# Attention and feed-forward kernel: the first batch's scales, exps and loads rearranged

## The chip, the cores and the metric

The kernel runs on one core of a Trainium2 chip. The core has five engines that run side by side, each through its own list of instructions in order: TensorE (PE in the profile, its weight loads PEld) multiplies matrices and writes to PSUM, VectorE (DVE) and ScalarE (ACT) read PSUM and work on tiles, GpSimd (POOL) works on tiles in SBUF alone here, and SyncE (SP) issues DMAs. ScalarE and GpSimd issue DMAs too; the profile marks an instruction in which an engine only issues as ACTq, POOLq or SPq. Engines wait for each other and for DMAs through semaphores.

The metric is device time in microseconds (us) of one execution; smaller is better.

## What is computed

The reference is a linear attention with an exponential feature map, followed by a gated feed-forward layer:

```python
batch, n_heads, seq, head_dim = (8, 8, 576, 64)
d_feat = 128
def phi(x):
    proj = np.einsum('bhsd,df->bhsf', x, w_phi)
    proj = proj - np.max(np.abs(proj), axis=-1, keepdims=True)
    return np.concatenate([np.exp(proj), np.exp(-proj)], axis=-1)
q_p, k_p = (phi(q), phi(k))
kv = np.einsum('bhsf,bhsd->bhfd', k_p, v)
z = np.sum(k_p, axis=2)
num = np.einsum('bhsf,bhfd->bhsd', q_p, kv)
den = np.einsum('bhsf,bhf->bhs', q_p, z)[..., None] + 1e-06
attn_out = (num / den).astype(np.float32)
x = np.ascontiguousarray(attn_out.transpose(0, 2, 1, 3)).reshape(B * S, H * D)
gate = np.maximum(x @ w_gate, 0.0)
val = x @ w_val
out = (gate * val @ w_out).astype(np.float32)
```

There are 4608 tokens, a model width of 512 and a hidden width of 1536. The row maximum that phi subtracts can be kept out of the big exps: the kernel computes exp(proj) and exp(-proj) from PSUM, and puts exp(-m) and exp(m), one number a row and sign, into v instead ("scales"). The column of ones that gives z becomes a column of the scales themselves.

## The kernel before, in words

**Tiles.** A batch has 8 heads of 576 rows: 512 rows in four chunks of 128, and a tail of 64 that is put together over heads, batches or both. A k item is two heads of one batch (four items a batch, `k_item`), plus one tail item (`k_tail`). For each item, pieces follow each other: kT (TensorE transposes k, VectorE copies it to SBUF as tT), krows (TensorE multiplies with w_phi, which lies twice in the tile w2, once for each half of the partitions), kmax (VectorE's row maximum, L247, and ScalarE's two small exps of it, the tile ek, L291), kexp (ScalarE's exps of the projection, the tile kp, L279), vs (GpSimd multiplies v by ek for both signs, L251, and casts ek into the last column, L257), and kv (TensorE sums over the rows, L323 and L331, with a copy to SBUF, L339). For the tail there is kmv in place of vs: GpSimd first makes ekm, ek with one half of the partitions zeroed (L308).

Queries go through qT, qrows (projection both ways round, L357 and L265), qexp (L372 to L375), qmax (row maximum and ScalarE's small cq, L385), num (TensorE times kv, L402, and five small VectorE steps up to a reciprocal r, with GpSimd's xu = u times r, L419) and x (a transpose of xu into xT). The feed-forward of batch g then runs in half steps: wv (L457, copied to val_sb by ScalarE, L466), wg (L457, joined by VectorE, L470), and at last out (L483). For the first batch a half step takes one chunk of 128 tokens and a third of the hidden width.

**Order.** Every piece is added to a plan with engine costs, needs and buffers, but what is emitted comes from ORDER, a list written into the file: numbers of pieces with the PSUM banks that they take, and entries such as z22:0, which stand for n times 128 columns of dummy matmuls on zeros (`keep_busy`, L999), into bank 0. The costs that stand beside the pieces are read by an ordering program that is not part of the kernel; `Plan.order` reads ORDER and nothing else. The order of the instructions on each engine, DMA issues included, is thus the order of ORDER, with the code ahead of it first. Piece 0 is the load of the first q, 1 and 2 the first thirds of the value and gate weights; 43 is the first kT.

**First loads.** Ahead of ORDER, SyncE issues two loads of k for heads 0 to 3 (in fp32), the k tail and the v tail; ScalarE issues one half of w_phi into wf and then v in four loads of two heads (L163); GpSimd issues the other half of w_phi straight into w2, makes the identity matrices, and loads k of heads 4 to 7 (late_k, in bf16, L1028). ScalarE then casts wf into w2 (L1036). Items 0 and 1 of the first batch run through `k_crosswise`: VectorE's maximum of one half of the heads beside ScalarE's exps of the other half.

```python
    for u in range(NU):
        if u < 2:
            load_kqv(0, "kn", k, nc.sync, FP32, slice(2 * u, 2 * u + 2))
        load_v(0, 2 * u, 2 * u + 2, nc.scalar)
    load_first_tail(0)
    load_tail(inputs["vt", 0], 0, 1, v, nc.sync)
```

Of the kernel before, what the change touches and what calls it, by code (L numbers as in the profile page):

```python
# [8 lines left out]
FP32 = mybir.dt.float32  # L9
# [37 lines left out]
ORDER = """z22:0 43:76 48:5 44:6 45 z6:4 49:0 z14:2 53:5 0 50 z12:4 54:2 65:7 3 59:6 4 56 1 5 z9:4 66:4 46 67  # L47
68 60:0 61 62 51 55 z56:7 70:4 77 69 84:5 52:6 63 71:02 72 7 11 73 47:7 z9:4 102:6 108:5 114:4 64:2
103:0 9 78:63 104 57 80 8 2 97:5 17 58:2 79 109:3 110 10 74:52 98:6 75:2 111 99 81:52 15 z15:3 76:4
105 82:3 126:2 120:5 85:03 87 139:2 100 86 533:7 88:53 121:0 525:2 6 83:7 89 90 541:2 122 16 526:7  # L50
13 115:3 527:5 101 106 152 123 107:2 18 170 116 117 91:67 168 112 124 528:5 542:7 171 92:6 113:0
94:51 95:2 535:7 543:6 127:30 129 536:7 118 12 128 544:2 177 130:50 96:7 93:3 131 534:4 119:2 125:7
140:53 14 132 142 529:2 133:70 539:1 162 134:4 136:32 537:0 141 538:7 530:1 545:0 189 137:7 20 546:4
21 143:52 153 144 163:0 145 531:7 547:4 164 135:2 19 552:3 166 165 138:5 172:6 173 540:2 553 149:45
554 167 169 150:0 146:12 183 175 174 548:5 549:4 532:3 154:60 155 550 156 147:5 551 221 184:2 22
190:0 178:6 555:5 556 558:4 186 179 180 229 191 185 557 559 187 151:6 192 148:7 157:23 176:5 560
561:3 158:76 195 196:40 197 567:2 24 583:3 181 193 188:6 198 208 159:7 182:4 23 223 241 160:5 562:0
199:61 200 242:3 201 194:5 243 563:0 25 26 584:1 568:2 244 28 575:7 230:5 224:0 222 565:2 573:3 231
225 205:47 566:2 574:3 235 226 232 564:7 206:4 577:2 260 202:30 245 273 576:1 579:7 203:2 227 580:0
236:5 289 209:31 238 211 204 578:7 233 585:0 210 569:1 237 570:2 591:7 291 207 29 212:53 213 239  # L60
581:1 214 571:2 33 298 572:3 215:45 582:6 228:1 246:2 247 30 218:35 240:1 219:4 592 216:2 234:1 283
220 593 292 248:53 284:1 249 217 586 587 310 250 304 588:7 251:35 285 290 252 594:0 595 253 589 286
27 254:65 596 257:34 255:5 590 597:6 598:4 258:7 603:5 287 305:0 342 307 256 261:26 31 263 613:4 262
161 306 609:5 604:6 316 308 614:7 615:4 299:0 264:26 265 266 610:5 605:4 356 300 34 601:6 302 301
274 602:7 35 616:5 259 270:62 32 309:3 617:4 267:75 271:0 618:1 607:6 272 608:2 599:7 311:0 329
275:35 313 277 600:2 611:7 276 312 288 619:5 303:6 606:2 394 620:7 268:0 612:1 293:2 317:46 295
624:0 318 627:1 269 628 319 294 625 320:62 321 357:4 412 410 314 629 626 343 322 296 358 278:23 344
297:6 279:71 350 315:0 39 280:3 639:6 359 323:20 630:1 37 360 637:3 326:07 324:6 631 345:4 351:2 38
347 632 362 352 621:0 327:7 622 635:6 623 281:1 325 633:7 346 634:6 638:0 353 419 354 640:1 330:46
331 653:0 332 645:1 348 654:2 36 646:3 355:0 333:16 363:4 334 335 636:3 647:0 643:6 413 42 364  # L70
339:73 328 644:2 411 365 649:6 361:3 648:7 366 340:0 336:12 655:6 651:7 425 337:0 381 395 349:5 341
652:6 396:13 426:5 397 641:7 398 427 656:0 663:4 642:7 368 428 367:3 650:2 414:0 369:52 664 666:7
338 416 463 667 41 431 370 665 371 689:2 668 420:5 515 422 415 372:03 374 373 421 657:2 660:7 450
661 691:3 669:4 378:56 423 375:01 376:3 662 658 379:4 40 659 687:1 404 399:03 670:2 690:1 405:6
382:42 407 477 417 384 683:0 671:1 429 406 383 692:2 688:3 408 400:01 681:2 684:3 672:1 675:2 385:64
432:0 386 673:3 424:2 387 433 434 682:4 418:5 377 388:36 465 679:7 674:2 464 677:4 391:30 437 389:1
380 676:2 685:7 680:0 471 430:1 435 392:7 686:6 409 390 393 678:5 483 478:3 480 438:60 693:2 694 439
699:5 440 436:0 695 484:6 479 282 441:30 481 700 702:2 442 443 701 485 696:0 486 705:1 703 401:3
447:45 444:67 697 402:1 704 445:3 698 709:7 706:4 707:5 472:6 451:02 474 453 708:4 452 516 710:5
719:2 473 448:3 482:4 713:5 723:0 454:61 466:3 502 456 489 455 724:5 720:0 446 717:1 467 711:2 714:5  # L80
457:01 460:67 449 468 475 469 712:2 715:5 458:1 487 461:0 718:3 470:4 727:7 490:15 491 716:4 732:0
725:7 492 733 488:1 721:2 476:1 493:35 462 459 494 728:7 729:2 726:1 722:7 403 730 495 738:1 496:73
731 745:4 497:3 498 499:56 747:2 743:7 734 500:6 503:24 735:7 741:0 736 504 739 740 505 737 506:52
742:4 746:7 744:0 507 508 748:1 509:45 510:0 749:6 751:7 750:3 759:2 760:1 512:07 513:6 752:5 757:4
753:7 761:6 755:0 758:7 756:1 517:24 518 519 768:0 763:1 501 511 771:7 754:6 762:5 764:4 769 774:3
514 520:21 775 521:65 522:4 765:1 772 776 770 777:2 799:6 766 781:0 767 773 779:0 778:6 800:7 780:5
523:6 787:4 782:7 788:3 793:2 783:1 784:0 794:7 524 797:6 789:5 791:7 798:6 785:0 792:7 813:1 790:0
786:2 795:1 804:0 801:7 796:6 802 805 806 810:1 807:2 803 811 823:0 812 817:3 808 809 829:7 814:6
818:5 824:7 815:6 816:0 827:7 819:1 828:0 835:2 830:1 821:0 836:7 831:6 820:5 822:7 833:6 834:0
825:7 826:1 832:0 837:2 838 846:3 839 847:7 843:6 848:7 840:5 841 844 845 842"""  # L90
# [6 lines left out]
def kernel(  # L97
# [23 lines left out]
    P = 128  # L121
# [55 lines left out]
    def load_tail(t, b, nb, src, eng):  # L177

        for hh in range(2):
            for bb in range(nb):  # L180
                eng.dma_start(
                    out=t[SM * hh : SM * (hh + 1), bb],
                    in_=src[b + bb, hh::2, SF:S, :].rearrange("u p d -> p u d"),
                )
# [64 lines left out]
    def scale_v(dst, src, ek):  # L249

        nc.gpsimd.tensor_tensor(  # L251
            dst[:, :, :, 0:D],
            src[:, :, None, :].to_broadcast([P, *dst.shape[1:3], D]),
            ek[:, :, :, None].to_broadcast([P, *dst.shape[1:3], D]),
            op=ALU.mult,
        )
        nc.gpsimd.tensor_copy(dst[:, :, :, D], ek)  # L257
# [15 lines left out]
    def k_exps(st, n, at, pars=slice(0, 2)):  # L273

        if "kp" not in st:
            st["kp"] = st["pool"].tile([P, 2, 2, 4, F], BF16, name="kp")
        kp = st["kp"][:, :, :, at : at + n]
        for s, sign in ((0, 1.0), (1, -1.0)):
            nc.scalar.activation(kp[:, s, pars], st["rows"][:, pars], AF.Exp, scale=sign)  # L279

    def k_max(st, n, pars=slice(0, 2)):

        if "m" not in st:
            st["m"] = sb_s.tile([P, 8], FP32, name="mk")[:, 0 : 2 * n]
        m = st["m"].rearrange("p (j i) -> p i j", i=2)
        row_max(m[:, pars], st["rows"][:, pars])

    def k_scales(st, n):
        st["ek"] = sb_s.tile([P, 8, 2], FP32, name="ek", bufs=8)[:, 0 : 2 * n]
        for s, sign in ((0, -1.0), (1, 1.0)):  # L290
            nc.scalar.activation(st["ek"][:, :, s], st["m"], AF.Exp, scale=sign)  # L291

    def k_crosswise(st):

        for par in range(2):
            k_max(st, 4, slice(par, par + 1))
            k_exps(st, 4, 0, slice(1 - par, 2 - par))
        k_scales(st, 4)

    def k_values(st, b, u):  # L300
        vs = st["vs"] = sb_k.tile([P, 8, 2, E], BF16, name="vs")
        vn = inputs["vn", b][:, 2 * u : 2 * u + 2].rearrange("p h c d -> p (h c) d")
        scale_v(vs, vn, st["ek"])

    def k_values_tail(st, b, at):

        ekm = sb_s.tile([P, NU, 2, 2], FP32, name="ekm", bufs=2)
        nc.gpsimd.tensor_tensor(  # L308
            ekm,
            st["ek"][:, at : at + NU, :, None].to_broadcast([P, NU, 2, 2]),  # L310
            half[:, None, None, :].to_broadcast([P, NU, 2, 2]),
            op=ALU.mult,
        )
# [3 lines left out]
    def k_kv(st, b, u, copy):  # L317
# [21 lines left out]
        copy(kv.rearrange("p h s e -> p (h s e)"), pk[:, 0 : 4 * E])  # L339
# [265 lines left out]
    def k_pieces(rank, st, start, ops, needs, take, name, banks, late=(), n=4, at=0, wide=True):  # L605
# [12 lines left out]
        if wide:  # L618
            wide_pieces(rank, st, n, at)
            return  # L620
# [3 lines left out]
            lambda: k_crosswise(st),  # L624
            [
                ("DVE", 0.6),
                ("ACT", 0.48, None),
                ("ACT", 0.48, None),
                ("DVE", 0.6, 2),
                ("ACT", 0.48, 0),  # L630
                ("ACT", 0.48, 0),
                ("ACT", 0.21, 3),
            ],
            [(rank, "proj")],
            (rank, "rows", 0),
            free=[((rank, "proj"), 5)],
        )

    def wide_pieces(rank, st, n, at, done=lambda: None):
# [506 lines left out]
```

## Time and profile before

| what | value |
|---|---|
| median of 8 runs | 390.37 us (389.66 to 390.83) |
| the profiled execution | 390.44 us |
| its span, first to last instruction | 388.7 us |
| mean granted TensorE clock | 0.996 |
| filler matmuls (L999) | 39, all between 1.0 and 32 us |
| HBM read, written | 37.81 MB, 9.44 MB |

Times inside the profile count from the span's start; 1.74 us of the execution lie around it. A row of the timeline reads: start, length, engine, line, operation, tile written and tiles read, count, and in brackets how long the engine had been idle before it and what released it. In the table of windows each stretch has its length, then for each of the engines PE, PEld, DVE, ACT and POOL the busy time with the number of instructions, and at the end the granted clock, the share of the DMA engines and GB/s. A busy TensorE can be busy with dummy matmuls, so the filler has to be taken off where useful work is asked for.

### The profile page before, as it was taken

How to read it: one execution, taken by the hardware profiler on the slowest of the kernel's cores; microseconds unless marked ns; L12 is line 12 of the kernel's file. 1: busy time of each engine (PE TensorE's matmuls, PEld its weight loads, DVE VectorE, ACT ScalarE, POOL GpSimd, SP SyncE). 2: the span in 40 equal slices, each digit the busy share in tenths (PEclk: the TensorE clock that was granted, in tenths of full speed). 3: DMA queues.
4: the chain of work that ended last, by engine and by line, in shares of the span. 5: the costliest groups of instructions: out<-in, count | busy, mean ns of one | idle time of the engine just before them, and what ended most of it. 6: DMA issues, size and time to landing. Idle time of an engine off the chain costs nothing.

```text
span 388.7 us, 8993 instructions
## 1 busy us (share of the span) xinstructions
PE 375.9 (97%) x3611; PEld 210.1 (54%) x3611; DVE 239.8 (62%) x413; ACT 239.9 (62%) x479; POOL 157.0 (40%) x178
## 2 busy tenths in 40 slices
PE   6979999999999999999999999999999999999994
PEld 3566898665465454645545465545545454444452
DVE  2697888868865778777746876577437443322330
ACT  2858868798858868778675767586463513413311
POOL 6797855685771684564305526236021101000000
PEclk9998999999999999999999999999999999999999
DMA  8999998999999796999383332210222011002003
GB/s 196 208 249 188 188 219 122 176 217 217 158 122 167 171 187 82 181 226 165 51 138 78 115 70 69 82 28 2 42 75 74 15 40 70 14 29 81 1 15 95
DMA packets 92506, 44.94 MB, mean 116 GB/s; under 512 B 58352, under 2 KB 87984, under 8 KB 92464
## 3 DMA queue, kind: packets, MB, share of 16 engines
q1 hardware_dynamic: 62352, 28.98, 34.4%
q0 software_dynamic: 28464, 13.78, 27.9%
q10 hardware_dynamic: 1648, 1.61, 1.3%
q8 instruction: 28, 0.46, 0.5%
q14 instruction: 14, 0.11, 0.1%
HBM read 37.81 MB, written 9.44 MB: 122 GB/s over the span
## 4 chain that ended last, share of the span: by engine, by line
PE 95%; DMA 1%; ACT 1%; DVE 1%; ACTq 0%; issue 0%; SPq 0%; DVEq 0%
PE pall L457 49%; PE pall L483 23%; PE pall L402 5%; PE pall L265 5%; PE pall L323 4%; PE pall L357 3%; PE pall L999 2%; DMA kt<-in_k_dram 1%; PE pall L240 1%; PE pall L331 1%; PE pall L510 1%; PE pall L429 0%; ACT qp L372 0%; DVE h L470 0%; DVE mq L247 0%; ACT val_sb L466 0%
## 5 line engine op out<-in xcount | busy, mean ns | idle before, releaser
L470 DVE SCALAR_TENSOR_TENSOR h<-pall,val_sb 128x512 bf16<-128x512 f32 x108 | 73.8, 686 | 74.9 <-PE pall L457 67.3
L466 ACT CAST val_sb<-pall 128x512 bf16<-128x512 f32 x108 | 63.5, 597 | 59.0 <-PE pall L457 47.5
L483 PE MATMUL pall<-wo_sb,h 128*128 128x512 bf16 x420 | 99.9, 379 | 0.0
L457 PE MATMUL pall<-xT,wv_sb 128*128 128x512 bf16 (+1 forms) x528 | 95.1, 321 | 0.5 <-ACT val_sb L466 0.5
L457 PE MATMUL pall<-xT,wg_sb 128*128 128x512 bf16 (+1 forms) x528 | 94.0, 321 | 0.0
L419 POOL TENSOR_TENSOR xu<-u,r 128x512 bf16<-128x512 f32 x36 | 37.4, 1043 | 125.3 <-DVE r L417 87.0
L251 POOL TENSOR_TENSOR vs<-vn,ek 128x1024 bf16<-128x1024 f32 x32 | 61.0, 1905 | 38.0 <-ACT ek L291 31.6
L279 ACT ACTIVATE kp<-pall 128x1024 bf16<-128x1024 f32 (+1 forms) x78 | 70.4, 966 | 8.9 <-PE pall L265 7.7
L457 PEld LDWEIGHTS <-wv_sb 128*128 128x128 bf16 x576 | 47.0, 98 | 41.7 <-issue 0.6
L457 PEld LDWEIGHTS <-wg_sb 128*128 128x128 bf16 x576 | 46.6, 98 | 40.1
L483 PEld LDWEIGHTS <-h 128*128 128x128 bf16 x420 | 38.6, 98 | 42.0
L247 DVE TENSOR_REDUCE mq<-pall 128x8 f32<-128x1024 f32 x36 | 43.8, 1220 | 17.1 <-PE pall L265 13.5
L247 DVE TENSOR_REDUCE mk<-pall 128x8 f32<-128x1024 f32 (+1 forms) x39 | 43.7, 1133 | 5.7 <-PE pall L265 3.7
L493 ACT COPY out_sb<-pall 128x512 f32<-128x512 f32 x35 | 20.4, 589 | 40.7 <-PE pall L483 37.5
L411 DVE TENSOR_TENSOR t<-pall,cq 128x455 f32<-128x455 f32 (+3 forms) x80 | 33.5, 419 | 17.6 <-PE pall L402 16.8
L374 ACT ACTIVATE qp<-pall 128x512 bf16<-128x512 f32 x60 | 36.7, 612 | 3.7 <-PE pall L357 3.7
L414 DVE TENSOR_TENSOR u<-pall,t 128x455 f32<-128x455 f32 (+3 forms) x80 | 34.2, 428 | 6.5
L375 ACT ACTIVATE qp<-pall 128x512 bf16<-128x512 f32 x60 | 37.2, 619 | 0.0
L402 PEld LDWEIGHTS <-qp 128*128 128x128 bf16 x640 | 27.2, 98 | 11.6 <-issue 1.2
L402 PE MATMUL pall<-kv,qp 128*128 128x65 bf16 x640 | 29.7, 194 | 1.2 <-DVE u L414 0.9
L323 PE MATMUL pall<-vs,kp 128*128 128x65 bf16 x512 | 20.7, 193 | 0.6 <-ACT val_sb L466 0.6
L323 PEld LDWEIGHTS <-kp 128*128 128x128 bf16 x512 | 18.8, 97 | 4.0 <-issue 0.7
(69 smaller groups left out, 272.6 us busy)
## 6 DMA issues: line engine op xcount, KB each, us to landing
out_dram<-out_sb SPq DMA_DIRECT2D x32, 256.0 KB, 2.3
vn<-in_v_dram SPq DMA_DIRECT2D x7, 1024.0 KB, 6.9
qn<-in_q_dram POOLq DMA_DIRECT2D x8, 512.0 KB, 8.4
kn<-in_k_dram POOLq DMA_DIRECT2D x7, 512.0 KB, 8.5
wv_sb<-in_moe_w_val_dram POOLq DMA_DIRECT2D x3, 512.0 KB, 13.3
wg_sb<-in_moe_w_gate_dram POOLq DMA_DIRECT2D x3, 512.0 KB, 10.6
wo_sb<-in_moe_w_out_dram POOLq DMA_DIRECT2D x3, 512.0 KB, 10.8
vn<-in_v_dram ACTq DMA_DIRECT2D x4, 256.0 KB, 5.6
```

The costliest lines, as they stand in the source:

```text
L247: nc.vector.tensor_reduce(m, banks, axis=AX.X, op=ALU.max, apply_absolute_value=True)
L251: nc.gpsimd.tensor_tensor(dst[:, :, :, 0:D], src[:, :, None, :].to_broadcast([P, *dst.shape[1:3], D]), ek[:, :, :, None].to_broadcast([P, ...
L279: nc.scalar.activation(kp[:, s, pars], st["rows"][:, pars], AF.Exp, scale=sign)
L323: nc.tensor.matmul(kv_ps[:, hh, s, :], lhsT=st["kp"][:, s, c % 2, 2 * hh + c // 2], rhs=st["vs"][:, 4 * hh + c, s, :], start=(hh == s == c ...
L374: nc.scalar.activation(x["qp"][:, s, a], cols[:, 0], AF.Exp, scale=sign)
L375: nc.scalar.activation(y["qp"][:, s, b], cols[:, 1], AF.Exp, scale=sign)
L402: nc.tensor.matmul(banks[s][:, i], lhsT=x["qp"][:, s, slot, P * blk : P * (blk + 1)], rhs=kvs[b, h // 2][:, h % 2, s, :],)
L419: nc.gpsimd.tensor_tensor(x["xu"], x["u"][:, :, 0:D], r.to_broadcast([P, 8, D]), op=ALU.mult)
L457: nc.tensor.matmul(ps[:, n * i : n * (i + 1)], lhsT=w[:, dc, P * fi : P * fi + P], rhs=xT[:, dc, lo:hi], start=(dc == 0), stop=(dc == NDC ...
L466: nc.scalar.copy(st["val", step], ps)
L470: nc.vector.scalar_tensor_tensor(st["h2"][:, fis[0] : fis[-1] + 1, lo:hi], ps.rearrange("p (a b) -> p a b", b=n), 0.0, st["val", step].rea ...
L483: nc.tensor.matmul(st["po", t], lhsT=st["h2"][:, fi, P * t : P * t + P], rhs=wo_sb[:, fi, :], start=(fi == 0), stop=(fi == NFC - 1),)
```

## The change

In the first batch (b = 0) all four k items take the wide form: one row maximum over both halves and one exp for each sign, each sign a piece of its own; `k_crosswise` is gone. ScalarE writes the scales twice there: into ek, and as bf16 straight into the last column of the v tile, so that GpSimd's cast of ek is left out. For the first tail ScalarE writes ekm itself, four small exps with a bias of 0 or -1e30 a partition, which takes the place of ek, of its two small exps and of GpSimd's multiplication by half. The copies of the first batch's kv go from VectorE to ScalarE. Other batches keep their operations.

The first loads are issued anew: SyncE takes v in three loads (2, 2 and 4 heads), mixed with the k and tail loads; ScalarE issues only w_phi, once for each half of wf, and casts all of it to w2; GpSimd begins with late k in one load, and after the identities copies one column of k's second load (held), so that what it issues later waits for that load. The two-batch tail loads (`load_tail` with nb = 2) take one DMA a half instead of two. ORDER is written anew throughout: 855 pieces instead of 849, 96 filler units of 128 columns instead of 143. The costs that stand beside the pieces change as well.

```diff
-ORDER = """z22:0 43:76 48:5 44:6 45 z6:4 49:0 z14:2 53:5 0 50 z12:4 54:2 65:7 3 59:6 4 56 1 5 z9:4 66:4 46 67
-68 60:0 61 62 51 55 z56:7 70:4 77 69 84:5 52:6 63 71:02 72 7 11 73 47:7 z9:4 102:6 108:5 114:4 64:2
-103:0 9 78:63 104 57 80 8 2 97:5 17 58:2 79 109:3 110 10 74:52 98:6 75:2 111 99 81:52 15 z15:3 76:4
-105 82:3 126:2 120:5 85:03 87 139:2 100 86 533:7 88:53 121:0 525:2 6 83:7 89 90 541:2 122 16 526:7
...
+ORDER = """z22:0 43:01 z1:2 50:2 44:0 z6:3 51:6 54 0 45 z5:5 64:5 46 52 z4:4 71:4 57:5 4 z23:3 72:2 53 47 58:4
+48 3 55 65:6 73 74 75 66 8 67 59 7 68 56:0 69 60 61 z4:1 76:1 49:2 90:3 62 77:60 78 63:3 70:2 83 79
+91:40 1 2 94:62 93 92 95 96 80:01 9 120:4 5 81:5 z7:2 103:3 6 z9:2 100:42 84:06 85 101:5 z2:3 82:3
+z13:2 104:4 106 86 11 114:2 531:3 105 102:0 17 532:1 87:67 121:2 115:4 108:0 117 10 537:1 107 553:7
...
         for hh in range(2):
-            for bb in range(nb):
-                eng.dma_start(
-                    out=t[SM * hh : SM * (hh + 1), bb],
-                    in_=src[b + bb, hh::2, SF:S, :].rearrange("u p d -> p u d"),
-                )
+            eng.dma_start(
+                out=t[SM * hh : SM * (hh + 1)],
+                in_=src[b : b + nb, hh::2, SF:S, :].rearrange("b u p d -> p b u d"),
+            )
...
-    def scale_v(dst, src, ek):
+    def scale_v(dst, src, ek, z=True):
...
         )
-        nc.gpsimd.tensor_copy(dst[:, :, :, D], ek)
+        if z:
+            nc.gpsimd.tensor_copy(dst[:, :, :, D], ek)
...
-    def k_exps(st, n, at, pars=slice(0, 2)):
+    def k_exps(st, n, at, signs=(0, 1)):
         if "kp" not in st:
             st["kp"] = st["pool"].tile([P, 2, 2, 4, F], BF16, name="kp")
         kp = st["kp"][:, :, :, at : at + n]
-        for s, sign in ((0, 1.0), (1, -1.0)):
-            nc.scalar.activation(kp[:, s, pars], st["rows"][:, pars], AF.Exp, scale=sign)
-
-    def k_max(st, n, pars=slice(0, 2)):
+        for s in signs:
+            nc.scalar.activation(kp[:, s], st["rows"], AF.Exp, scale=(1.0, -1.0)[s])
+
+    def k_max(st, n):
         if "m" not in st:
             st["m"] = sb_s.tile([P, 8], FP32, name="mk")[:, 0 : 2 * n]
         m = st["m"].rearrange("p (j i) -> p i j", i=2)
-        row_max(m[:, pars], st["rows"][:, pars])
+        row_max(m, st["rows"])
     def k_scales(st, n):
         st["ek"] = sb_s.tile([P, 8, 2], FP32, name="ek", bufs=8)[:, 0 : 2 * n]
         for s, sign in ((0, -1.0), (1, 1.0)):
             nc.scalar.activation(st["ek"][:, :, s], st["m"], AF.Exp, scale=sign)
-
-    def k_crosswise(st):
-
-        for par in range(2):
-            k_max(st, 4, slice(par, par + 1))
-            k_exps(st, 4, 0, slice(1 - par, 2 - par))
-        k_scales(st, 4)
+        if "z" in st:
+            vs = st["vs"] = sb_k.tile([P, 8, 2, E], BF16, name="vs")
+            for s, sign in ((0, -1.0), (1, 1.0)):
+                nc.scalar.activation(vs[:, :, s, D], st["m"], AF.Exp, scale=sign)
+
+    def k_scales_halves(st):
+
+        st["ekm"] = sb_s.tile([P, NU, 2, 2], FP32, name="ekm", bufs=2)
+        for s, sign in ((0, -1.0), (1, 1.0)):
+            for hh in range(2):
+                nc.scalar.activation(
+                    st["ekm"][:, :, s, hh], st["m"], AF.Exp, scale=sign, bias=other[:, hh : hh + 1]
+                )
     def k_values(st, b, u):
-        vs = st["vs"] = sb_k.tile([P, 8, 2, E], BF16, name="vs")
+        if "z" not in st:
+            st["vs"] = sb_k.tile([P, 8, 2, E], BF16, name="vs")
         vn = inputs["vn", b][:, 2 * u : 2 * u + 2].rearrange("p h c d -> p (h c) d")
-        scale_v(vs, vn, st["ek"])
+        scale_v(st["vs"], vn, st["ek"], "z" not in st)
     def k_values_tail(st, b, at):
-        ekm = sb_s.tile([P, NU, 2, 2], FP32, name="ekm", bufs=2)
-        nc.gpsimd.tensor_tensor(
-            ekm,
-            st["ek"][:, at : at + NU, :, None].to_broadcast([P, NU, 2, 2]),
-            half[:, None, None, :].to_broadcast([P, NU, 2, 2]),
-            op=ALU.mult,
-        )
+        ekm = st.get("ekm")
+        if ekm is None:
+            ekm = sb_s.tile([P, NU, 2, 2], FP32, name="ekm", bufs=2)
+            nc.gpsimd.tensor_tensor(
+                ekm,
+                st["ek"][:, at : at + NU, :, None].to_broadcast([P, NU, 2, 2]),
+                half[:, None, None, :].to_broadcast([P, NU, 2, 2]),
+                op=ALU.mult,
+            )
         vs = vts[b] = sb_mix.tile([P, NU, 4, E], BF16, name=f"vsm{b % 2}")
         scale_v(vs, inputs["vt", b // 2][:, b % 2], ekm.rearrange("p u s h -> p u (s h)"))
-    def k_kv(st, b, u, copy):
+    def k_kv(st, b, u):
...
-        copy(kv.rearrange("p h s e -> p (h s e)"), pk[:, 0 : 4 * E])
+        nc.scalar.copy(kv.rearrange("p h s e -> p (h s e)"), pk[:, 0 : 4 * E])
...
+        us = 0.08 + n * 0.206
+        if "z" in st:
+            for s in range(2):
+                plan.add(
+                    rank,
+                    "kexp",
+                    lambda s=s: k_exps(st, n, at, (s,)),
+                    [("ACT", us)],
+                    [(rank, "proj")],
+                    (rank, "exps", s),
+                    free=[((rank, "proj"), 0, 3)],
+                )
             return
...
-        st = {"pool": sb_k}
+        st = {"pool": sb_k} if b else {"pool": sb_k, "z": True}
...
-            lambda: k_kv(st, b, u, nc.scalar.copy if b else nc.vector.tensor_copy),
+            lambda: k_kv(st, b, u),
...
+    other = singles.tile([P, 2], FP32)
...
-    nc.scalar.dma_start(out=wf[0:D], in_=w_phi)
-    nc.gpsimd.dma_start(out=w2[D:P], in_=w_phi)
...
-    for u in range(NU):
-        if u < 2:
-            load_kqv(0, "kn", k, nc.sync, FP32, slice(2 * u, 2 * u + 2))
-        load_v(0, 2 * u, 2 * u + 2, nc.scalar)
+    nc.gpsimd.dma_start(
+        out=late_k, in_=k[0, 4:8, 0:SF, :].rearrange("h (p c) d -> p h c d", c=C)
+    )
+    for u in range(2):
+        load_kqv(0, "kn", k, nc.sync, FP32, slice(2 * u, 2 * u + 2))
+        nc.scalar.dma_start(out=wf[D * u : D * (u + 1)], in_=w_phi)
+    load_v(0, 0, 2)
     load_first_tail(0)
-    load_tail(inputs["vt", 0], 0, 1, v, nc.sync)
+    load_v(0, 2, 4)
+    load_v(0, 4, 8)
+    load_tail(inputs["vt", 0][:, 0:1], 0, 1, v, nc.sync)
     make_identity(nc, ident[FP32])
     nc.gpsimd.tensor_copy(ident[BF16], ident[FP32])
-    for u in range(2):
-        nc.gpsimd.dma_start(
-            out=late_k[:, 2 * u : 2 * u + 2],
-            in_=k[0, 4 + 2 * u : 6 + 2 * u, 0:SF, :].rearrange("h (p c) d -> p h c d", c=C),
-        )
+    held = singles.tile([P, 1], FP32)
+    nc.gpsimd.tensor_copy(held, inputs["kn", 0][:, 2, 0, 0:1])
+    nc.scalar.copy(w2, wf)
     nc.vector.memset(half, 0.0)
+    nc.vector.memset(other, -1e30)
     for hh in range(2):
         rows = slice(D * hh, D * (hh + 1))
         nc.vector.memset(half[rows, hh : hh + 1], 1.0)
-    nc.scalar.copy(w2[0:D], wf[0:D])
+        nc.vector.memset(other[rows, hh : hh + 1], 0.0)
```

## The prediction

> **What bounds the kernel now.** I read the page first (busy time and the slices), then busy time in windows, then TensorE's waits, then the timeline of the first 36 us, and last DMA landings and the shapes of ScalarE's work.
>
> ```profile
> span 388.7 us, 8993 instructions
> PE 375.9 (97%) x3611; PEld 210.1 (54%) x3611; DVE 239.8 (62%) x413; ACT 239.9 (62%) x479; POOL 157.0 (40%) x178
> ```
>
> TensorE is busy 97% of the span, so only its idle time and its dummy work can be won. The dummy work is the filler of line 999: 39 matmuls, 12.7 us, all before 32 us. Real work is therefore 375.9 - 12.7 = 363.2 us. The windows (PE busy is the first figure after the length) say where the idle time sits:
>
> ```profile
> 6.00:8.00 2.00, 0.00 (x0) 0.00 (x0) 0.49 (x1) 0.30 (x1) 1.56 (x3) 1.00 1.11 221
> 24.00:26.00 2.00, 1.48 (x29) 1.28 (x27) 2.00 (x2) 0.31 (x2) 2.00 (x5) 1.00 1.22 290
> 26.00:28.00 2.00, 0.98 (x22) 0.87 (x22) 2.00 (x5) 1.87 (x3) 2.00 (x4) 1.00 1.43 202
> 28.00:30.00 2.00, 0.88 (x19) 0.68 (x19) 1.83 (x6) 2.00 (x5) 0.55 (x2) 1.00 1.27 208
> 30.00:32.00 2.00, 1.97 (x14) 0.93 (x11) 1.53 (x3) 1.79 (x5) 1.62 (x2) 0.58 1.24 206
> 140.00:200.00 60.00, 59.51 (x587) 31.57 (x584) 43.47 (x72) 45.19 (x88) 29.69 (x34) 1.00 0.99 142
> ```
>
> From 6 to 8 us TensorE does nothing, from 24 to 30 us it is idle 2.66 us, and after 45 us only 0.49 us is lost, apart from some 5 us of last stores. So the change is worth what it saves in the first batch, provided that nothing new opens later. The timeline names the chain:
>
> ```profile
> 3.71 0.37 ACTq L163 DMA_DIRECT2D vn<-in_v_dram  x1
> 7.29 0.37 ACTq L163 DMA_DIRECT2D vn<-in_v_dram  x1
> 7.70 0.30 ACT L1036 CAST w<-wf 64x128 bf16<-64x128 f32 x1 [5.47 <-DMA kt<-in_k_dram]
> 8.05 0.61 PE L265 MATMUL pall<-w,tT 64*128 64x128 bf16 x8 [2.29 <-ACT w L1036]
> 11.04 1.90 POOL L251 TENSOR_TENSOR vs<-vn,ek 128x1024 bf16<-128x1024 f32 x1 [3.48 <-ACT ek L291]
> 22.42 1.94 POOL L251 TENSOR_TENSOR vs<-vn,ek 128x1024 bf16<-128x1024 f32 x1
> 34.69 1.06 PE L457 MATMUL pall<-xT,wv_sb 128*128 128x128 bf16 x16
> ```
>
> ScalarE issues the loads of v and then casts w_phi, in order. Its third v load goes out at 3.71 us, when the first k load lands (0.73 + 3.0), and its fourth at 7.29, just after a k tail lands (1.75 + 5.5). Both sit where eight SyncE and ScalarE loads are under way. So the cast waits until 7.70 although w_phi landed at 0.97 + 2.9 = 3.9, and TensorE waits 2.29 us for it. GpSimd's first product then starts at 11.04 and its last of the batch at 22.42, with 1.30 us idle after the first, five casts of 0.25 us and two DMA issues (0.95 + 0.77) in between. The first FFN step comes at 34.69.
>
> **What the Trainium skill says.** "TensorE: Matmul & The Clock Gate", Part 1, says that TensorE runs at half its clock until it has been busy for about 3.4 us. The trace agrees: 512-column fillers take about 420 ns at the start and 229 ns at 15 us, and the granted clock falls to 0.58 at 30 us, after the gap. "DMA: Bandwidth & Descriptors", Issuing engines are not separate DMA queues, says that another issuing engine saves only the sequencer's time. So moving v to SyncE doesn't make it land sooner; what it frees is ScalarE. I took no price from these two. "ScalarE: Activation LUTs", Rules for kernel authors, gives about 0.3 us for an ACTIVATE plus 0.83 ns an element. The trace has 0.22 us for 128x8, and in a row these start about 0.1 us apart; 128x1024 start 0.905 us apart (two from 26.24 to 28.05). I use the trace. No page that I know of bears on the eight loads.
>
> **Part by part.** Only ORDER, the loads and the operations count: the program is emitted in ORDER's sequence, and the changed planner costs are read by nothing.
>
> *Loads.* ScalarE now issues only two w_phi loads, at 0.97 and 1.63. The second lands about 2.9 later, at 4.55, and the cast ends near 4.9. On SyncE nine loads stand in a row at 0.5 to 0.7 us each: k 0.73 and 1.26, v 1.75, two tails, v 3.5, v 4.0, two tails 4.5 and 5.1. v heads 0-1 should land near 6.5, as now. Late k goes out from GpSimd near 1.3, 1.5 us sooner than now. Cost on the path: nothing, covered by the fp32 transposes (3.82 to 5.9). If late k held back k's second load, I take 0.3 us at most.
>
> *First rows.* TensorE's rows of item 0 need the cast and the copied transposes (VectorE ends at 5.37 now). Behind item 1's transposes they stand at 5.9 instead of 8.05. Item 1's rows end near 7.7.
>
> *ScalarE.* It gets eight z exps (8 x 0.1 = 0.8 us), two more for the tail (0.2) and four kv copies (4 x 0.30 = 1.2), and eight 512-wide exps at 0.48 become four at 0.905 (-0.2). That is +2.0 us on an engine that has about 6 us idle between 8 and 26 us. In the new order: exp of item 1 7.7-8.6, scales of item 0 to 9.0, exp 9.9, scales of item 1 10.5, two exps 12.3, tail scales 12.7, tail exps 13.7, item 3's scales 14.1, exp 15.0, item 2's scales 15.4, exp 16.3, kv copy 16.6, two exps 18.4, kv copy 18.7, q exps of chunk 0 20.5, two kv copies and cq 21.2, q exps of the pair (2 x 1.92) 25.05.
>
> *GpSimd.* The casts of the first batch go (5 x 0.25 = 1.25) and so does the 0.21 of ekm. Products at 1.85 each: 9.2-11.05, 11.05-12.9, tail 12.9-14.8, item 3 16.65, item 2 18.5. The last ended at 24.36; that is 5.9 us sooner. The new wait on the second k load (held) delays only q0's issue, from 4.28 to about 4.7. Moved behind the products are the issues of wv0 and wv1 (6.03 and 6.8 now, 18.5 and about 21 then). Four tail DMAs a pair become two, for 2.48 us of GpSimd at 25 us and 3.19 of SyncE at 41; no wait there ends on the path, so I count nothing.
>
> *First FFN step.* The last kv copy is at 21.1. Chunk 0's nums on VectorE (0.62 + 0.63 + 0.22 + 0.23 + 0.20, behind two row maxima of 1.22) end at 24.8, xu (1.04) at 25.8. On TensorE a num of the pair stands ahead, which needs ScalarE's 25.05; VectorE's part of it ends at 27.7, the xT copy (0.42) at 28.1. The step starts at 28.2 instead of 34.7: 6.5 us.
>
> *What has been done by then.* The new order leaves for later two k transposes (0.5), two k rows (0.8), two q transposes (1.04 + 0.62) and chunk 1's num (0.9), and has done one more q rows (0.8) and a num (0.9): 2.2 us less real work. Net 4.3 us. The sum has no semaphore hops: ek to GpSimd is 0.08 and r to GpSimd 0.09 in the trace; 14 such hops at 0.1 are an estimate of 1.4 us. Left: 2.9. Later stages I take as equal: ScalarE then owes four items of k exps beside the FFN's 0.6 us casts, some 10 us against some 11.7 of TensorE's work, where 1.06 us is lost now too.
>
> The profiled execution took 390.44 us (388.7 span + 1.74), 0.07 above the median of 390.37. 390.44 - 2.9 = 387.5.
>
> **Rivals.**
> - *ScalarE becomes the bound of the head.* For it: my row has it full from 7.7 to 25 us. Against it: 6 us idle now, and the small exps overlap. If each of the ten extra exps costs 0.22 instead of 0.1 (+1.2) and the order slips another 0.8, 2 us of the 2.9 go: 389.5. That the cast comes no earlier because loads still block gives nearly the same.
> - *The head falls more.* If hops are hidden and the gap of 1.06 after 36 us closes too: 390.44 - 4.3 - 1.0 = 385.1. For it: late k and the tails come earlier. Against it: such rows on paper are always too short.
> - *The weights come late (slower).* For it: their issue stands behind the last product, at 18.5, and now they take 13.3 (wv0) and 15.3 us (wv1) to land. With these, wv0 lands at 31.8 and wv1 at 36.3, where FFN steps want them at 28.2 and near 33. It decides once a weight is over 2.9 us late. Five more loads follow at the present spacing of about 3 us (wv0 19.3, wv1 22.1), so the lag adds up; 4.4 us late gives 390.44 + 1.5 = 391.9. Against it: the long landings are of loads queued behind q0 and k1; at 18.5 us the queue should be nearly empty, so wv0 lands near 23.5.
>
> **How the numbers follow.** Forecast (386.0 to 389.2) 0.50; ScalarE bound 0.20; falls more 0.10; weights late 0.20. 0.2% (0.8 us) is about what can be told from no change, so faster is below 389.6. Faster: 0.47 + 0.12 + 0.10 + 0.01 = 0.70; same: 0.02 + 0.05 + 0.02 = 0.09; slower 0.21. The range takes in the second and third case and the edge of the last: 385.0 to 391.3.
>
> **What would show it.** Right: the w_phi cast by 5.2 us, first rows of TensorE near 6, GpSimd's last product of the batch ending near 18.5, fillers under 10 us, the first FFN step near 28 to 30. Wrong: TensorE waiting for a wv or wg load, ScalarE without a pause from 8 to 30 us while VectorE and GpSimd wait for it, or new idle time after 45 us.

## The result and the profile after

The changed kernel takes 387.18 us (median of 12 runs, 384.66 to 391.36) against 390.16 of the kernel before (median of 33): ratio 0.9915, 95% interval 0.9899 to 0.9932. That is 3.0 us less, where 2.9 had been forecast. One of the 12, the 391.36, counts as a slow run and is left out of the ratio. The executions of the changed kernel lie much further apart than those of before, and the profiled one is among its faster ones: 386.33 us, a span of 384.5. So the two traces differ by 4.1 us where the medians differ by 3.0.

From the page of the changed kernel:

```profile
span 384.5 us, 8954 instructions
PE 371.2 (97%) x3601; PEld 208.3 (54%) x3601; DVE 237.1 (62%) x410; ACT 240.9 (63%) x489; POOL 151.7 (39%) x166
```

TensorE is busy 4.7 us less. Its filler (L1005 now) is 9.64 us in 29 matmuls instead of 12.70 in 39, and the same 3572 other matmuls take 361.55 us instead of 363.2, because fewer of them run at half clock. Idle time is 13.4 instead of 12.8. So -3.06 - 1.65 + 0.6 = -4.1: idle time was not saved in sum. The windows of the changed kernel, in the columns of those shown before, say where it went:

```profile
6.00:8.00 2.00, 0.04 (x2) 0.04 (x3) 0.42 (x1) 0.30 (x1) 0.34 (x1) 1.00 1.02 221
16.00:18.00 2.00, 0.00 (x0) 0.10 (x1) 1.15 (x2) 2.00 (x8) 2.00 (x3) 1.00 1.20 313
28.00:30.00 2.00, 1.85 (x28) 1.44 (x29) 1.87 (x5) 1.00 (x3) 1.70 (x2) 1.00 1.26 212
30.00:32.00 2.00, 2.00 (x29) 1.39 (x27) 1.93 (x6) 2.00 (x4) 1.47 (x3) 1.00 1.23 202
140.00:200.00 60.00, 60.00 (x615) 32.41 (x614) 42.41 (x71) 46.55 (x95) 28.10 (x30) 1.00 0.92 140
```

The hole from 6 to 8 us is still there. There is a new one at 16 us. The hole at 28 us and the half clock at 30 us are gone. The timeline of the changed kernel, with TensorE's longest waits (total, times, longest) after it, shows what the first two wait for:

```profile
7.61 0.30 ACT L1038 CAST w<-wf 128x128 bf16<-128x128 f32 x1 [5.38 <-DMA wf<-in_w_phi_dram]
11.21 3.76 POOL L251 TENSOR_TENSOR vs<-vn,ek 128x1024 bf16<-128x1024 f32 x2 [4.87 <-ACT ek L292]
15.86 1.90 POOL L251 TENSOR_TENSOR vsm<-vt,ekm 128x1024 bf16<-128x1024 f32 x1 [0.89 <-ACT ekm L303]
17.87 3.75 POOL L251 TENSOR_TENSOR vs<-vn,ek 128x1024 bf16<-128x1024 f32 x2
31.20 1.06 PE L467 MATMUL pall<-xT,wv_sb 128*128 128x128 bf16 x16
35.02 1.90 POOL L251 TENSOR_TENSOR vsm<-vt,ekm 128x1024 bf16<-128x1024 f32 x1
```

```profile
PE pall L341 <- POOL vsm L258: 2.3, 1, 2.3
PE pall L266 <- ACT w L1038: 2.3, 1, 2.3
```

ScalarE is free of the v loads, and yet the cast starts at 7.61, against 7.70 before: it waits for the second w_phi load itself, which was issued at 1.6 us and took 5.9. GpSimd's first product starts at 11.21, no sooner than before. What has become shorter is the way from there to the last product of the batch: it ends at 21.62 instead of 24.36. Two DMA issues (0.95 and 0.77 us) stood between the products before the change and stand behind them now; that move, the wide exps, the kv copies on ScalarE and the new order of the head (the part up to the first feed-forward step) were not tested alone.

The first feed-forward step follows at 31.20, 3.5 us sooner, with less other work done by then (13.3 us of real TensorE work instead of 15.7). What is left from that step on is shown here for the kernel before and then for the changed kernel:

```profile
34.69:388.70 354.01, 347.48 (x3313) 192.26 (x3310) 217.01 (x368) 218.34 (x434) 131.12 (x141) 1.00 0.59 106
31.20:384.50 353.30, 348.21 (x3343) 193.33 (x3340) 219.11 (x374) 219.19 (x438) 132.95 (x143) 1.00 0.63 110
```

By its busy time, TensorE has 0.7 us more left to do (30 matmuls), and not the 2.4 us between 13.3 and 15.7. The other 1.7 us is the same work done in less time: the kernel before ran at half clock from 30.33 to 33.74 us, just ahead of its first step. So the head gives about 3.5 - 0.7 = 2.8 us, and the part from the first step on the other 1.3: TensorE's idle time there falls from 6.5 to 5.1 us.

The clock column needs a caution. The clock record of a trace begins with the first rise to full clock, at 13.26 us before the change and 13.06 after it, and for the time ahead of that the windows print 1.00. But up to 12.9 us 512-column fillers of the changed kernel start 427 ns apart, and from 13.2 us on 216: up to 13 us both kernels ran at half clock.

### The profile page after: what moved, and what is told of

Same layout as the page of the kernel before. It is cut to its first block, busy times and chain, and to the rows that moved or that the text cites. A ratio compares the mean times of both kernels' runs of the same rounds, so it can differ in the third digit from the quotient of the medians.

```text
span 384.5 us, 8954 instructions
## 1 busy us (share of the span) xinstructions
PE 371.2 (97%) x3601; PEld 208.3 (54%) x3601; DVE 237.1 (62%) x410; ACT 240.9 (63%) x489; POOL 151.7 (39%) x166
## 4 chain that ended last, share of the span: by engine, by line
PE 90%; ACT 4%; DMA 4%; POOL 1%; issue 0%; DVE 0%; ACTq 0%; SPq 0%; POOLq 0%
PE pall L467 48%; PE pall L493 23%; PE pall L412 5%; PE pall L266 4%; PE pall L333 4%; PE pall L367 3%; DMA vn<-in_v_dram 2%; DMA wf<-in_w_phi_dram 2%; PE pall L1005 1%; ACT kp L280 1%; PE pall L341 1%; PE pall L240 1%; PE pall L520 1%; ACT qp L385 1%; POOL vs L251 0%; ACT qp L382 0%
## 5 line engine op out<-in xcount | busy, mean ns | idle before, releaser
L467 PEld LDWEIGHTS <-wg_sb 128*128 128x128 bf16 x576 | 47.4, 98 | 41.7
L384 ACT ACTIVATE qp<-pall 128x512 bf16<-128x512 f32 x60 | 37.1, 618 | 5.8 <-PE pall L367 5.7
L385 ACT ACTIVATE qp<-pall 128x512 bf16<-128x512 f32 x60 | 37.6, 626 | 0.0
L412 PE MATMUL pall<-kv,qp 128*128 128x65 bf16 x640 | 30.5, 194 | 1.0 <-ACT qp L385 0.5
```

What stands on the lines that cost most here:

```text
L384: nc.scalar.activation(x["qp"][:, s, a], cols[:, 0], AF.Exp, scale=sign)
L385: nc.scalar.activation(y["qp"][:, s, b], cols[:, 1], AF.Exp, scale=sign)
L412: nc.tensor.matmul(banks[s][:, i], lhsT=x["qp"][:, s, slot, P * blk : P * (blk + 1)], rhs=kvs[b, h // 2][:, h % 2, s, :],)
L467: nc.tensor.matmul(ps[:, n * i : n * (i + 1)], lhsT=w[:, dc, P * fi : P * fi + P], rhs=xT[:, dc, lo:hi], start=(dc == 0), stop=(dc == NDC ...
```

## The experiments

Twelve further kernels, each timed against the kernel before. An interval of a ratio is some 0.3% wide either way, about 1 us, so effects of half a microsecond are not told apart by time; there I go by the traces.

| kernel | median us | ratio (95%) |
|---|---|---|
| changed | 387.18 | 0.9915 (0.9899 to 0.9932) |
| latek_after_ident | 387.04 | 0.9903 (0.9865 to 0.9941) |
| latek_after_held | 390.39 | 0.9996 (0.9976 to 1.0015) |
| gpsimd_casts | 387.09 | 0.9897 (0.9865 to 0.9928) |
| v_on_scalar | 388.85 | 0.9948 (0.9917 to 0.9979) |
| w_by_gpsimd | 386.79 | 0.9931 (0.9907 to 0.9956) |
| tail_scales_first | 387.42 | 0.9933 (0.9907 to 0.9958) |
| filler_in_gap | 386.96 | 0.9917 (0.9897 to 0.9936) |
| w_by_gpsimd_filler | 385.48 | 0.9877 (0.9848 to 0.9906) |
| after_loads_first | 393.84 | 1.0071 (1.0041 to 1.0101) |
| before_cast_first | 392.10 | 1.0062 (1.0050 to 1.0074) |
| before_products_first | 389.55 | 0.9980 (0.9968 to 0.9993) |
| before_cast_and_products | 387.91 | 0.9935 (0.9912 to 0.9959) |

**Why w_phi is still late.** Two kernels move the issue of late k on GpSimd:

```diff
-    nc.gpsimd.dma_start(out=late_k, ...)          # ahead of all other loads
     nc.gpsimd.tensor_copy(ident[BF16], ident[FP32])
+    nc.gpsimd.dma_start(out=late_k, ...)          # latek_after_ident
     nc.gpsimd.tensor_copy(held, inputs["kn", 0][:, 2, 0, 0:1])
+    nc.gpsimd.dma_start(out=late_k, ...)          # latek_after_held, instead
```

> Changed kernel, but GpSimd issues late k after the identities (near 2.2 us instead of 1.26). Theory A: late k, 256 KB into the same DMA engines, is what delays the second w_phi load (issued 1.6, landed 7.5). Then that load lands before 6.5 us, the cast starts a us or more before 7.61, TensorE's wait of 2.27 us for it shrinks as much, and the time falls by 0.5 to 1.5 us from 387.2. Theory B: the second w_phi load is slow because it stands behind the k and v loads of SyncE, whatever GpSimd does: the cast stays at 7.6 within 0.3 us and the time within 0.5 us of 387.2.

> Changed kernel, but GpSimd issues late k only after k's second load has landed (near 4.6 us instead of 1.26). Theory A: the second w_phi load lands near 4.5, the cast ends near 5, TensorE's first rows start near 6 instead of 7.96; late k itself lands near 10 to 11, which may hold the transposes of items 2 and 3 (10.3 now). Time 1 to 2 us below 387.2 if late k holds nothing, about equal if it does. Theory B: the cast stays at 7.6 and the time is not below 387.0.

The second w_phi load took 5.9 us with late k first, 5.2 with late k after the identities and 3.9 with late k held back; the casts started at 7.6, 6.9 and 5.6. With the loads left as in the changed kernel the cast came between 6.7 and 7.6 in the other experiments, so the middle step alone shows nothing and the last one does: theory A holds for w_phi. The time did not follow it in either kernel. Held back, late k itself kept TensorE waiting 5.1 us, and the kernel was as slow as before the change. One delayed load had been exchanged for another on the same DMA engines.

The next kernel loads one half of w_phi through GpSimd into w2, as before the change, and lets late k follow the identities:

```diff
+    nc.scalar.dma_start(out=wf[0:D], in_=w_phi)
+    nc.gpsimd.dma_start(out=w2[D:P], in_=w_phi)
-        nc.scalar.dma_start(out=wf[D * u : D * (u + 1)], in_=w_phi)
-    nc.scalar.copy(w2, wf)
+    nc.scalar.copy(w2[0:D], wf[0:D])
```

> Changed kernel with w_phi loaded as before the change (one half by ScalarE, the other straight into w2 by GpSimd, whose late k then follows the identities). Theory A: with v off ScalarE and no second w_phi load on its queue, both halves land by 4.7 us, the cast ends near 4.5, TensorE's first rows start near 6 instead of 7.96, GpSimd's first product near 9 instead of 11.2, and the time falls by 1 to 2 us from 387.2. Theory B: the v load (8.65) or late k takes the place of w_phi, the first product stays later than 10.5 and the time within 0.5 us of 387.2.

From the timeline of w_by_gpsimd, ScalarE's cast having started at 3.9:

```profile
8.35 1.90 POOL L251 TENSOR_TENSOR vs<-vn,ek 128x1024 bf16<-128x1024 f32 x1 [1.88 <-ACT ek L292]
11.98 1.90 POOL L251 TENSOR_TENSOR vs<-vn,ek 128x1024 bf16<-128x1024 f32 x1 [1.73 <-ACT ek L292]
15.11 1.90 POOL L251 TENSOR_TENSOR vsm<-vt,ekm 128x1024 bf16<-128x1024 f32 x1 [1.23 <-ACT ekm L303]
17.12 3.75 POOL L251 TENSOR_TENSOR vs<-vn,ek 128x1024 bf16<-128x1024 f32 x2
```

The first product is 2.9 us earlier than in the changed kernel and the last one 0.75 us: of the early start three quarters are lost in two waits on the way (TensorE stood 2.0 us for late k). The first feed-forward step came at 30.45, 0.75 us sooner; the time is not distinguishable from that of the changed kernel. The head has several waits of nearly the same length one behind the other, and removing one uncovers the next; that is how I read a trace that has what theory A says and a time that has what theory B says.

**v on ScalarE again**, the first thing that the change did away with (`nc.scalar` in the three `load_v` calls, behind the w_phi loads):

> Changed kernel, but ScalarE issues the three v loads of the first batch again, behind its two w_phi loads and ahead of the cast. Theory A: since the cast waits for the second w_phi load until 7.5 us anyway, moving v off ScalarE won nothing by itself: the time stays within 0.5 us of 387.2. Theory B: the issues block on the loads in flight as they did before the change, the cast comes at 8 us or later and the time rises by 0.5 us or more.

The cast started at 9.0, as theory B has it. The median rose by 1.7 us, but the two intervals overlap a little, and in its trace TensorE ran at half clock for 17 us from 8.59 us on (8.59 to 15.41, 18.82 to 29.07). Moving v off ScalarE thus kept the cast from getting later, which is not what I had thought; that it pays in time is likely and not quite shown.

**The casts on GpSimd again:**

```diff
-            for s, sign in ((0, -1.0), (1, 1.0)):
-                nc.scalar.activation(vs[:, :, s, D], st["m"], AF.Exp, scale=sign)
-        scale_v(st["vs"], vn, st["ek"], "z" not in st)
+        scale_v(st["vs"], vn, st["ek"])
```

> Changed kernel, but GpSimd casts the scales of the first batch's items into v (L258), and ScalarE's eight small exps into v are left out. Theory A: GpSimd's products set when the first feed-forward step starts, so four casts at about 0.2 us delay it by 0.5 to 0.8 us, and the time rises by as much. Theory B: ScalarE bounds the head; freed of eight small exps it gets faster, and the time falls by 0.3 to 0.8 us.

From the start of the first product to the end of GpSimd's last piece the batch took 11.0 us (10.52 to 21.56) instead of 10.4: the casts cost 0.6 us there, as expected. The time didn't move, neither up nor down; w_phi came 0.7 us sooner in this execution and covered it. Undecided in time. Scales put into v by ScalarE are worth at most about 1 us, the width that this measurement can't see.

**The tail's scales, and the new hole at 16 us.** In ORDER, piece 73 goes ahead of 47 and z23 becomes z8; in the other kernel z36:1 stands ahead of the first kv (56):

> Changed kernel with the tail's row maximum and scales ahead of the last big exp of item 0 on ScalarE, and the filler ahead of the tail's rows cut from 23 units to 8. Theory A: GpSimd's tail product (15.86) waits for ScalarE's four small exps, which stand behind a big exp; moved ahead, the product starts near 15.0, GpSimd's last product ends 0.7 to 0.9 us earlier, TensorE's wait of 2.3 us for the tail shrinks by as much, and the time falls by 0.5 to 1.0 us from 387.2. Theory B: the first feed-forward step is set by ScalarE's q exps (busy to 28 us), which come no earlier: the time stays within 0.3 us.

> Changed kernel with 36 units of filler ahead of the first kv, where TensorE stands idle from 15.7 to 18.0 us. Theory A: the wide spread of the changed kernel (384.7 to 391.4 against 389.7 to 391.2 for most runs before) comes from TensorE's clock, which falls in some executions after this gap; with the gap filled the spread narrows to about 1 us and the median falls by 1 to 2 us. Theory B: the spread comes from when the first loads land; filler changes nothing, or costs up to 1 us where it runs at half clock ahead of the kv matmuls.

With its scales first the tail product started at 15.63, but by now waited for the DMA of v's tail; the time stayed. Filler alone didn't move the median either (386.96), and its six runs still lie between 385.18 and 387.92, wider than theory A has it.

The clock itself can be read from the traces. With the time ahead of the first rise counted at half clock, six profiles of the changed kernel and its variants have a mean of 0.76 to 0.92 over the first 27 us and spans of 384.0 to 385.3, and four have 0.57 to 0.71 and spans of 388.1 to 392.1. In three of these four, waits that the edit itself brought add to it. The fourth is tail_scales_first: its last product ended at 21.4 us as usual, but the first feed-forward step came at 33.80. Two windows of its trace, then two of the changed kernel's:

```profile
13.13:16.54 3.41, 1.41 (x34) 1.02 (x33) 2.88 (x3) 3.22 (x8) 2.57 (x2) 1.00 1.38 215
16.54:26.78 10.24, 8.99 (x97) 7.01 (x98) 3.02 (x5) 8.62 (x22) 7.85 (x8) 0.50 0.80 173
13.06:16.47 3.41, 2.19 (x41) 1.45 (x39) 2.41 (x4) 3.38 (x9) 2.52 (x3) 1.00 1.40 201
16.47:19.88 3.41, 1.87 (x37) 1.70 (x36) 1.37 (x2) 3.41 (x13) 3.41 (x4) 1.00 1.10 335
```

Why these windows: in each of the 14 traces the changes of the clock inside the span lie whole multiples of 3.41 us apart. I cut every trace into such stretches, from its first rise to 12 us before its end. TensorE was idle for 1.68 us or more in 15 stretches at full clock, and 14 of them were followed by half clock; the other, with 1.88 us, was not. No stretch with 1.65 us or less was followed by half clock. The hole at 16 us in the changed kernel is 2.35 us long, but it lies across a boundary, and leaves 1.22 and 1.54 us of idle time on the two sides; in tail_scales_first 2.00 us fall into one stretch. The half clock at 30.33 us before the change follows 1.75 us in four small holes. So in these traces it is where a hole falls in the stretches that decides whether it costs clock, and they begin at another time in each execution. That fits the wide spread of the changed kernel; that it makes all of it isn't shown.

**Both together**, w_phi as in w_by_gpsimd and the filler:

> Changed kernel with w_phi loaded as before the change and 36 units of filler in TensorE's gap ahead of the first kv. Theory A: the two gains (first feed-forward step 0.75 us earlier each, alone) share the same slack, and the filler keeps the clock: median 386.0 to 386.8, no execution above 388.5. Theory B: filler runs at half clock and delays kv: median 387.0 or more.

385.48 us, all five runs between 384.59 and 387.02: below both kernels, and better than I had expected. Its interval still touches that of the changed kernel. In its trace full clock begins at 4.38 us instead of 13.06 and lasts to the last microsecond; TensorE is fully busy from 27 to 32 us and the first feed-forward step comes at 30.06.

**The kernel before, with the cast put first.** This takes away the 2.29 us wait with which my prediction began, and nothing else:

```diff
     for u in range(NU):
+        if u == 2:
+            nc.scalar.copy(w2[0:D], wf[0:D])
         load_v(0, 2 * u, 2 * u + 2, nc.scalar)
-    nc.scalar.copy(w2[0:D], wf[0:D])
```

> Kernel before the change, with the cast of w_phi put ahead of ScalarE's third and fourth v loads, and nothing else. Theory A: TensorE's wait of 2.29 us for the cast is the head of the chain that sets the first feed-forward step, so the cast comes near 4.0 to 5.0 us and the time falls by 1 to 2 us from 390.2. Theory B: v loads, late k or GpSimd's products, whose order is unchanged, hold the rest: the cast comes early but the time falls by less than 0.5 us.

The cast started at 4.0, the batch's last product ended at 21.6 instead of 24.4, the first feed-forward step came at 32.76 instead of 34.69, and the kernel got 2 us slower. Neither theory has that. Its GpSimd timeline, and the longest wait of its TensorE between 27 and 45 us:

```profile
30.22 0.74 POOL L172 DMA_DIRECT2D qm<-in_q_dram  x1 [2.23 <-DMA qn<-in_q_dram]
32.72 0.68 POOL L172 DMA_DIRECT2D qm<-in_q_dram  x1 [1.76 <-DMA wv_sb<-in_moe_w_val_dram]
35.37 0.82 POOL L215 DMA_DIRECT2D wg_sb<-in_moe_w_gate_dram  x1 [0.91 <-DMA kt<-in_k_dram]
38.16 1.90 POOL L251 TENSOR_TENSOR vsm<-vt,ekm 128x1024 bf16<-128x1024 f32 x1
```

```profile
PE pall L323 <- POOL vs L257: 2.8, 1, 2.8
```

GpSimd does not get to issue its next load until an earlier one has landed. Which one, the semaphores in the trace tell: GpSimd's loads report their landing on eight semaphores in turn, and the load that waits is one that takes over a semaphore whose last load is still under way. So the qm load at 32.72 waits for the wv load issued eight loads earlier, which landed at 32.44. SyncE's and ScalarE's loads share eight other semaphores: in the kernel before, ScalarE's third and fourth v loads (3.71 and 7.29) took over those of the first k load (landed 3.69) and of a k tail (7.26). It is a wait in the program's own instructions; no trace here shows a full queue. GpSimd's products of the second batch stand behind these issues, at 38.16, where they were before the edit too (38.04). An earlier head only makes TensorE stand longer: 2.8 us at the second batch's kv, with the clock at 0.50 from 27 to 32 us. The kernel before has the same blocks, shorter, in its own GpSimd waits from 18 to 50 us:

```profile
POOL qm L172 <- DMA wv_sb<-in_moe_w_val_dram: 1.1, 1, 1.1
POOL wg_sb L215 <- DMA kt<-in_k_dram: 0.6, 1, 0.6
```

The changed kernel has none. That gave a new theory, and three kernels for it: pieces 101 and 106 (tail product and first product of the second batch) ahead of load 15 in the order before; the same with the cast first; and, in the changed kernel, the opposite (each piece leaves its old place further on):

```diff
-111 99 81:52 15 z15:3 76:4
+111 99 81:52 101 106 15 z15:3 76:4
...
-115:4 108:0 117 10 537:1 107 553:7
+115:4 108:0 117 10 537:1 15 14 12 13 107 553:7
```

> Kernel before the change, with GpSimd's tail product and first product of the second batch put ahead of the loads qm0, wg1, k2 and wo1 in its order, and nothing else. Theory A: near 31 to 38 us GpSimd stands at loads that wait for earlier loads to land, and the second batch's products (38.04 and 40.04) wait behind them; moved ahead they start near 31 and 33 us, TensorE's waits between 36 and 44 us (1.6 us idle) go, and the time falls by 0.5 to 1.5 us from 390.1. Theory B: ScalarE and VectorE set that stretch: the products come earlier, the time stays within 0.4 us.

> Kernel before the change with both edits: the cast of w_phi ahead of ScalarE's third v load, and the second batch's first products ahead of the loads. Theory A: the early cast alone cost 2 us because TensorE ran 2.7 us sooner into products that GpSimd held back behind loads (a wait of 2.8 us, and a fallen clock); with the products ahead of the loads that wait goes and the time falls to 387.5 to 389.5. Theory B: the early head starves TensorE for another reason (loads land no sooner, fillers too short for the clock): the time stays above 390.5.

> Changed kernel with GpSimd's loads qm0, wo2, wo0 and wo1 put ahead of the second batch's tail product, as loads stood before the change. Theory A: GpSimd then waits for earlier loads to land before it may issue, the tail product starts at 38 us or later instead of 35.02, TensorE gets idle time between 36 and 50 us where it has none now, and the time rises by 1 us or more from 387.2. Theory B: the loads are issued without a wait and the time stays within 0.5 us.

All three went as theory A has it, the first at the low end of what it says. Alone, the order of GpSimd gives 0.2% (interval 0.07 to 0.32%); with the cast first it gives 387.91, that is 4.2 us less than the cast alone. In that trace the tail product and the next start here:

```profile
28.11 1.90 POOL L251 TENSOR_TENSOR vsm<-vt,ekm 128x1024 bf16<-128x1024 f32 x1
30.10 1.90 POOL L251 TENSOR_TENSOR vs<-vn,ek 128x1024 bf16<-128x1024 f32 x1
```

The clock was 0.50 from 27 to 32 us there as well, so this fall does not set the two kernels apart; the blocked GpSimd does. Part of what it cost came through the clock all the same: behind the wait of 2.8 us before_cast_first ran at half clock once more, from 42.44 to 45.85 us, and this kernel did not. In the changed kernel with its loads first, GpSimd waits again and its tail product moves from 35.02 to 42.51, 1.9 us of it by the wait and 3.9 by the five issues themselves:

```profile
41.45 0.74 POOL L222 DMA_DIRECT2D wo_sb<-in_moe_w_out_dram  x1 [1.94 <-DMA qn<-in_q_dram]
42.51 1.90 POOL L251 TENSOR_TENSOR vsm<-vt,ekm 128x1024 bf16<-128x1024 f32 x1
```

TensorE then stands 3.1 us for an xu that GpSimd makes behind the tail product. The median is 393.84, 6.7 us above the changed kernel. Part of this is the clock: in its trace TensorE ran at half clock from 15.91 to 26.15 us, ahead of the place of the edit, and again from 46.63 to 50.05, behind the new wait. From the first feed-forward step on that execution took 359.3 us against 353.3.

## Why the prediction came out right

The time was right, 2.9 us forecast and 3.0 measured. The prediction had the whole gain ahead of the first feed-forward step, and in the profiled pair that part did give about 2.8 us. But two terms of its sum were wrong by nearly the same amount, and that they cancelled is luck. The part behind that step, put at nothing, gave 1.3 us more; the profiled pair lies 4.1 us apart, and no trace shows how the 3.0 of the medians are divided.

*Loads.* The second w_phi load was put at 2.9 us, the duration of the first; it took 5.9. I had allowed 0.3 us for late k moving ahead of k and had not seen that w_phi and v stand behind it too: v's first load landed at 8.7 us and not near 6.5. The cast did not end near 4.9 but at 7.9, TensorE's first rows came at 7.96 and not 5.9. That the cast comes no earlier stood in the prediction only as the last sentence of a rival.

*ScalarE and GpSimd.* The products started 2.0 us later than forecast (11.21 for 9.2) and ended 3.1 later (21.62 for 18.5), since the wait for w_phi remained and the tail product waited 0.89 us for ScalarE's four exps. Held delayed q0's issue to 4.55 (4.7 forecast).

*First feed-forward step.* It came 3.5 us sooner; the forecast was 6.5 less 1.4 for hops, so 1.6 us too much.

*What has been done by then.* The work left for later was put at 2.2 us and is 0.7, so 1.5 us too much the other way. The prices came from the trace of before, some of them from its stretch at half clock: eight transposes of q took 1.04 us at 32.28 and 0.62 at 34.24, and the sum has both. The prediction also took the trace to agree that half clock ends after about 3.4 us of work; in this trace it lasted to 13.26 us, though TensorE had been busy from 0.99 to 5.77 but for 0.3 us.

*Later stages.* "Equal" failed. The 1.5 us of waits between 36 and 200 us went down to 0.1. The second rival had named the gap of 1.06 us after 36 us, and it did close. I had read the loads that GpSimd issues there as work of 0.7 to 0.9 us each, without an end that anybody waits for. The profile had shown the mark: two of them with a DMA as releaser. The experiments of the last group show that the order of products and loads on GpSimd acts here; how much of the 1.3 us comes from it is not separated. In the kernel before it was worth 0.2% alone, and 4.2 us behind an earlier cast.

*Rivals.* The weights were not late: issued at 21.57, the first landed 5.8 us later, near the 5 that I had reckoned for an empty queue, and 3.9 us before its use. ScalarE was busy nearly throughout from 10 to 28 us, but freeing it of eight small exps (gpsimd_casts) did not shorten anything that could be measured.

## What to carry to other kernels

A load that an engine issues is not only as long as its issue: here it also waited for an earlier load to land, and every product behind it on that engine waited too. So look in the trace for issues with a DMA as releaser, and put the products that others need ahead of loads that can't start yet anyway. Test the removal of a wait alone before counting it: the longest wait of the head, taken away by itself, made this kernel slower, and with one more edit in the place where the gain got stuck, faster by more than 2 us. Don't take the price of work from a stretch at half clock when that work moves elsewhere. A small load can be as late as the large ones that were issued just ahead of it or beside it.

## What the runs showed of the hardware

Two loads of 32 KB, issued 0.6 us apart by the same engine, took 2.8 and 5.9 us; the second fell to 3.9 when a load of 256 KB from another engine was held back.

A GpSimd load was kept from issue for up to 2.2 us until an earlier one had landed, by a wait for the semaphore that it takes over.

TensorE's clock changed only at multiples of 3.41 us from its first rise. Of the stretches of that length at full clock, 14 of the 15 with 1.68 us or more of idle TensorE were followed by half clock, and none with 1.65 us or less. Matmuls of 512 columns started 427 ns apart at half clock and 216 at full clock.
